# The list of pieces of a fused attention and mixer kernel, ordered anew up to the channel feed-forward

## The chip, the cores and the metric

One core of one Trainium2 chip runs the whole computation as one launch. The metric is device time in microseconds (us) of that core. The kernel before takes 791.38 us, the median of three runs (790.44, 791.38 and 794.9). The engines are TensorE (PE in the rows; PEld is its loading of weights), VectorE (DVE), ScalarE (ACT), GpSimd (POOL) and SyncE (SP). Each takes its instructions in the order in which they were issued to it. SP issues every load and store here.

## What is computed

Attention over 4 batches of 8 heads (576 tokens, 64 dimensions) in two versions, added: a local one, in which a token sees the tokens nearer than 4, and one on means of 4 neighbouring tokens, repeated back to full length. Then a gated feed-forward over 512 channels (mixer 1), a rank-32 mixing of tokens with U and V, and a channel feed-forward with 2048 hidden channels. The weights of mixer 1 and the later ones arrive in double precision.

```python
out_d = sm_attn(q_d, k_d, v_d)                      # q_d, k_d, v_d: means of 4 tokens
mask = np.abs(pos[:, None] - pos[None, :]) < factor # factor = 4
attn = softmax(np.where(mask, scale * q @ k.T, -1e9))
x = np.repeat(out_d, factor, axis=2) + attn @ v     # then heads side by side: 512 channels
h = np.maximum(x @ w_in, 0.0)                       # mixer 1, d_ff = 1024
gate = 1.0 / (1.0 + np.exp(-conv3(h)))              # 3 taps along tokens, per channel
x = h * gate @ w_out
u = x + (x.T @ U @ V).T                             # tokens mixed, rank 32
out = u + np.maximum(u @ w_ch1, 0.0) @ w_ch2        # 4 * 512 hidden channels
```

## The kernel before

The 32 heads run as 16 pairs. For a pair p, q and k are loaded (L295), transposed on TensorE against a unit matrix (L355), copied out and summed over 4 tokens (L376, L386, L407, L417). Scores S come from L441 (mask) and L447, those of the means Sd from L470; their maxima from VectorE (L454, L480), exponentials from ScalarE (L461, L489), scaling of the softmax from GpSimd or VectorE (L504). P is transposed again (L516, L520), copied out (L529, L533), and multiplied with values: L551 takes vw, the values in windows, loaded by six transfers (L305 to L307) into a buffer that there is only once; L562 takes vd, sums of vr (loaded at L316, added on GpSimd at L427). VectorE adds both into x (L583).

Mixer 1 takes x in 6 blocks of 384 tokens and 8 groups of hidden channels: 48 products "1.n" (L793, twelve matmuls each, since every operand is split in a high and a low part), a relu on ScalarE (L804), the convolution (L823 on ScalarE, L829 on VectorE), tanh (L833), the gate (L838, split at L843 and L846), and the products back "2.n" (L855). Sums are evicted at L864. Then the token mix with U and V (L889 to L910), whose inputs are split at L871 and L875, and the channel feed-forward (L962 and L981, which fill the second half of the time).

A weight block is 512 KB of doubles. It is loaded (L323 or L325 for mixer 1), decoded in four steps (ScalarE L213, VectorE L215, L217, L220), and split (high part ScalarE L225, low part GpSimd or VectorE L229). U and V are loaded and decoded the same way through one spare buffer (L741 to L777): the second half of V (L768) can only be loaded when GpSimd has read the first (L777).

What sets the order is one string of 2570 words, CFG["SEQ"], from L22 on. The loop at L1024 to L1026 reads it word by word, and each word issues one piece on all the engines that it uses: "alq.9" loads q of pair 9, "alk" its k, "alw" vw, "alv" vr, "aqT" transposes, "aS" the scores, "wl.2" loads weight block 2, "wd.2" its next decode step, "wh.2" its high part, "wo.2" its low part on GpSimd and "wO.2" the same on VectorE, "1.0" the next three matmuls of product 1.0, "r1.0" its relu, "uv" the next step of U and V, "mi" and "mo" the token mix, "3.n", "4.n" the channel feed-forward. Engines wait for each other through semaphores that the framework sets; no scheduler moves anything. A word further ahead is thus an instruction further ahead in the queue of each engine that it uses.

Of the kernel before, what the change touches and what calls it, by code (L numbers as in the profile page):

```python
# [21 lines left out]
    SEQ="wl.2 wd.2 lc C wd.2 wd.2 wl.0 wd.2 wd.0 wh.2 alk.0 wd.0 wd.0 wd.0 wh.0 alq.0 aqT.0 wo.0 alv.0 avd.0 "  # L22
# [143 lines left out]
def mixer_kernel(ctx, tc, q, k, v, w_in, conv_w, w_out, mU, mV, w_ch1, w_ch2, out, stop=9, dbg=None, early_end=False):  # L166
# [856 lines left out]
    for name, (_, fn) in OPS.items():  # L1023
        ACTS["a" + name] = fn  # L1024
    for word in CFG["SEQ"].split():
        name, *at = word.split(".")  # L1026
# [30 lines left out]
```

## Time and profile before

| what | before |
|---|---|
| device time, median of 3 runs | 791.38 us |
| profiled execution, device time | 791.73 us |
| its span in the trace | 789.5 us |
| TensorE busy | 749.0 us, 95% |
| VectorE busy | 423.5 us, 54% |
| ScalarE busy | 343.7 us, 44% |
| GpSimd busy | 168.3 us, 21% |

The span runs from the first to the last recorded instruction. Busy time is summed over an engine's instructions. In the page's 40 slices of the span the figures are busy tenths, from left to right, about 19.7 us each; the row PEclk is the granted clock of TensorE in tenths of full speed:

```profile
PE   3767999999999999999999999999999999999998
DVE  6798896977887889899866511121221212112112
ACT  4777877857767666676444211111111110111110
POOL 3456546325323314112413100000000000000000
PEclk9578999999999999999999999999999999999999
```

The first four slices are attention without a product of mixer 1. From the fifth on attention and mixer 1 run together, from 271.3 us (the first L889) with the token mix, whose last L889 starts at 380.4 us; the rest is the channel feed-forward.

### The profile page before, as it was taken

The numbers are of one execution on the slowest core, as the hardware profiler recorded it, in microseconds if no ns is written. First come the engines' busy times: TensorE is split into PE (matmuls) and PEld (weight loads), VectorE is DVE, ScalarE is ACT, GpSimd is POOL, SyncE is SP. The second block draws the span as 40 slices with busy tenths as digits, with TensorE's granted clock in tenths as the row PEclk, the third lists the DMA queues.
The fourth block names the chain that finished last, engine by engine and source line by source line (L and its number), as shares of the span: only waits on it lengthen the run. The fifth ranks groups of instructions, "written<-read, shape, count | busy, mean of one in ns | idle before, by whom it ended". The sixth has DMA issues, their size and how long they took to land.

```text
span 789.5 us, 13123 instructions
## 1 busy us (share of the span) xinstructions
PE 749.0 (95%) x5061; PEld 665.2 (84%) x5061; DVE 423.5 (54%) x830; ACT 343.7 (44%) x1029; POOL 168.3 (21%) x237
## 2 busy tenths in 40 slices
PE   3767999999999999999999999999999999999998
PEld 3556888879888898987898988999899899999997
DVE  6798896977887889899866511121221212112112
ACT  4777877857767666676444211111111110111110
POOL 3456546325323314112413100000000000000000
PEclk9578999999999999999999999999999999999999
DMA  9967644253241302121234100010010001001001
GB/s 208 218 169 176 143 104 106 48 119 75 66 108 52 97 28 80 54 81 32 70 113 160 67 2 0 1 41 1 0 41 1 1 1 40 1 1 41 1 0 41
DMA packets 85458, 51.04 MB, mean 65 GB/s; under 512 B 62716, under 2 KB 79892, under 8 KB 85396
## 3 DMA queue, kind: packets, MB, share of 16 engines
q1 hardware_dynamic: 85396, 50.21, 24.5%
q8 instruction: 40, 0.66, 0.3%
q14 instruction: 22, 0.18, 0.1%
HBM read 45.47 MB, written 4.72 MB: 64 GB/s over the span
## 4 chain that ended last, share of the span: by engine, by line
PE 84%; DVE 8%; ACT 3%; DMA 2%; SPq 1%; issue 1%; POOL 1%; DVEq 0%; POOLq 0%; ACTq 0%
PE acc L981 25%; PE gb L962 13%; PE g L962 13%; PE acc L855 11%; PE g L793 9%; PE O L551 3%; PE gb L793 2%; PE tr L355 2%; PE Sd L470 1%; DVE hc L829 1%; PE O L562 1%; PE T L516 1%; PE h L889 1%; PE ut L948 1%; DMA qr<-in_q_dram 1%
## 5 line engine op out<-in xcount | busy, mean ns | idle before, releaser
L981 PE MATMUL acc<-w,a 128*128 128x512 f32 x864 | 216.0, 393 | 0.1
L981 PEld LDWEIGHTS acc<-w,a 128*128 128x128 f32 x864 | 160.7, 188 | 29.2 <-DVE a L971 0.6
L855 PE MATMUL acc<-w,ghl 128*128 128x512 f32 x432 | 112.8, 399 | 0.1
L962 PE MATMUL gb<-uT,w 128*128 128x384 f32 x576 | 111.4, 339 | 0.0
L962 PE MATMUL g<-uT,w 128*128 128x384 f32 x576 | 111.4, 339 | 0.0
L962 PEld LDWEIGHTS gb<-uT,w 128*128 128x128 f32 x576 | 101.7, 188 | 3.8 <-DVE a L971 0.2
L962 PEld LDWEIGHTS g<-uT,w 128*128 128x128 f32 x576 | 101.6, 188 | 3.7 <-DVE a L971 0.2
L971 DVE SCALAR_TENSOR_TENSOR a<-gb,a 128x384 fp32r<-128x384 f32 x48 | 26.7, 557 | 129.4 <-ACT a L970 129.3
L855 PEld LDWEIGHTS acc<-w,ghl 128*128 128x128 f32 x432 | 80.1, 190 | 17.1 <-DVE ghl L846 1.4
L793 PE MATMUL g<-xhl,w 128*128 128x386 f32 (+1 forms) x456 | 92.9, 346 | 0.2 <-ACT hc L804 0.2
L971 DVE SCALAR_TENSOR_TENSOR a<-g,a 128x384 fp32r<-128x384 f32 x48 | 26.7, 556 | 123.0 <-ACT a L970 123.0
L793 PEld LDWEIGHTS g<-xhl,w 128*128 128x128 f32 x456 | 80.5, 191 | 2.9 <-issue 0.7
L970 ACT ACTIVATE a<-g 128x384 fp32r<-128x384 f32 x48 | 23.5, 491 | 134.0 <-PE g L962 130.1
L970 ACT ACTIVATE a<-gb 128x384 fp32r<-128x384 f32 x48 | 23.5, 490 | 132.4 <-PE gb L962 123.7
L829 DVE SCALAR_TENSOR_TENSOR hc<-hc,cw 128x384 f32<-128x384 f32 x96 | 64.4, 672 | 13.2 <-ACT hc L823 11.1
L461 ACT ACTIVATE P<-S,nm 122x64 f32<-122x64 f32 x160 | 47.8, 319 | 5.4 <-DVE nm L454 5.1
L846 POOL TENSOR_TENSOR ghl<-hc,ghl 128x384 fp32r<-128x384 f32 x22 | 25.1, 1142 | 78.2 <-ACT ghl L843 62.4
L833 ACT ACTIVATE hc<-hc 128x384 f32<-128x384 f32 x48 | 25.2, 527 | 24.3 <-DVE hc L829 24.1
L843 ACT ACTIVATE ghl<-hc 128x384 fp32r<-128x384 f32 x48 | 25.1, 527 | 22.8 <-DVE hc L838 16.2
L551 PEld LDWEIGHTS O<-PT,vw 64*64 64x64 f32 x640 | 23.5, 149 | 12.4 <-DVE xd L572 2.7
L461 ACT ACTIVATION_READ_ACCUMULATOR P<-S,nm 122x1 f32 x160 | 33.9, 212 | 0.0
L551 PE MATMUL O<-PT,vw 64*64 64x58 f32 x640 | 27.1, 237 | 7.0 <-DVE xd L572 2.4
(129 smaller groups left out, 1008.2 us busy)
## 6 DMA issues: line engine op xcount, KB each, us to landing
wraw<-in_moe_w_ch_dram SPq DMA_DIRECT2D x29, 512.0 KB
kr<-in_k_dram SPq DMA_DIRECT2D x32, 144.0 KB
qr<-in_q_dram SPq DMA_DIRECT2D x32, 144.0 KB
vr<-in_v_dram SPq DMA_DIRECT2D x32, 144.0 KB
out_dram<-u SPq DMA_DIRECT2D x17, 256.0 KB
w1t<-in_moe_w_in_dram SPq DMA_DIRECT2D x8, 512.0 KB
w1t<-in_moe_w_out_dram SPq DMA_DIRECT2D x8, 512.0 KB
vw<-in_v_dram SPq DMA_DIRECT2D x32, 128.0 KB
```

What stands on the lines that cost most here:

```text
L461: nc.scalar.activation(out=e["P"][:, i, h], in_=e["S", h][:122, i], func=AF.Exp, bias=e["nm"][:, h, i:i + 1], accum_out=e["sm"][:, i, h:h ...
L551: nc.tensor.matmul(O[rows, c:c + QB], e["vw"][rows, 2 * i + a], PT[rows, i, 64 * a:64 * a + QB], start=True, stop=True)
L793: nc.tensor.matmul(p[:, :wd], w[:, a, cc], xhl[g, cc][:, b, :wd], start=k == 0, stop=k == 3 * NCC - 1)
L829: nc.vector.scalar_tensor_tensor(out=o, in0=inner(g, hts[n], k), scalar=cw[:, k * NF + f:k * NF + f + 1], in1=o, op0=ALU.mult, op1=ALU.add)
L833: nc.scalar.activation(out=cts[n], in_=cts[n], func=AF.Tanh)
L843: nc.scalar.activation(out=t[:, 0], in_=cts[n], func=AF.Copy)
L846: eng.tensor_tensor(ghl[n][:, 1], cts.pop(n), ghl[n][:, 0].bitcast(F32), op=ALU.subtract)
L855: nc.tensor.matmul(acc[g][c], t[:, a, c * P:(c + 1) * P], w[:, b], start=f == 0 and i == 0, stop=f == NF - 1 and i == 2)
L962: nc.tensor.matmul(p[:, :TB], w[:, a, cc], uT[g, cc][:, b, :TB], start=k == 0, stop=k == 3 * NCC - 1)
L970: nc.scalar.activation(out=t[:, 0], in_=p[:, :TB], func=AF.Relu)
L971: nc.vector.scalar_tensor_tensor(out=t[:, 1], in0=p[:, :TB], scalar=0.0, in1=t[:, 0].bitcast(F32), op0=ALU.max, op1=ALU.subtract)
L981: nc.tensor.matmul(acc2[g][c], t[:, a, c * P:(c + 1) * P], w[:, b], start=f == 0 and i == 0, stop=f == NF2 - 1 and i == 2)
```

## The change

Only the string differs. It holds the same 2570 words' worth of pieces, and from word 1959 on it is the same word by word; the first 1958 stand in a new order. In some places a piece that can go to one of two engines is given to the other: GpSimd is issued 228 instructions instead of 239, VectorE 842 instead of 831, ScalarE 821 as before. By line: low parts of weights (L229) on VectorE 26 instead of 21, low parts of the gate (L846) 29 instead of 26, low parts of the token mix's inputs (L875) 12 instead of 10. Buffers, the matmuls and their number are the same. The first line of the string, and the lines with the load of pair 9's vw ("alw.9"):

```diff
-    SEQ="wl.2 wd.2 lc C wd.2 wd.2 wl.0 wd.2 wd.0 wh.2 alk.0 wd.0 wd.0 wd.0 wh.0 alq.0 aqT.0 wo.0 alv.0 avd.0 "
+    SEQ="wl.0 wd.0 wd.0 lc C alq.0 aqT.0 wd.0 wd.0 alk.0 wh.0 aqc.0 wl.2 akT.0 akv.0 aqs.0 wl.1 aks.0 wd.2 wd.2 "
...
-        "aE0.11 avd.10 aE1.11 anv.10 akc.12 c1.12 th.12 2.10 2.10 2.9 2.10 andv.11 alk.14 gh.11 gL.11 alw.9 "
+        "aEd.11 2.6 alw.9 uv 1.10 1.10 1.10 1.10 akv.12 2.7 2.7 2.7 gh.8 gl.8 r1.10 aT1.9 axdv.8 axa.8 ax.8 avd.9 "
```

In the three places below a row is a line of the program, what it issues, and the tiles (out<-in). Numbers behind a tile's name tell its copies apart.

SP's queue from its first transfer on, before and then now. w1t is a weight block of mixer 1, craw the weights of the convolution, qr and kr are q and k of a pair, vr the values for the means:

```order
L325 DMA w1t_144<-in_moe_w_in_dram 128x4x256
L688 DMA craw_139<-in_moe_conv_w_dram 24x256
L325 DMA w1t_157<-in_moe_w_in_dram 128x4x256
L295 DMA kr_163<-in_k_dram 96x6x64 x2
L295 DMA qr_171<-in_q_dram 96x6x64 x2
L316 DMA vr_182<-in_v_dram 72x2x256 x2
L323 DMA w1t_190<-in_moe_w_out_dram 128x1024
L295 DMA qr_249<-in_q_dram 96x6x64 x2
L295 DMA kr_265<-in_k_dram 96x6x64 x2
```
```order
L325 DMA w1t_144<-in_moe_w_in_dram 128x4x256
L688 DMA craw_139<-in_moe_conv_w_dram 24x256
L295 DMA qr_156<-in_q_dram 96x6x64 x2
L295 DMA kr_168<-in_k_dram 96x6x64 x2
L325 DMA w1t_174<-in_moe_w_in_dram 128x4x256
L323 DMA w1t_188<-in_moe_w_out_dram 128x1024
L316 DMA vr_201<-in_v_dram 72x2x256 x2
L295 DMA kr_209<-in_k_dram 96x6x64 x2
L295 DMA qr_212<-in_q_dram 96x6x64 x2
```

The first q and k moved ahead of the second weight block, and q ahead of k.

VectorE's queue in the same part of the program, from the eviction of the convolution's weights (cw) on. L215, L217 and L220 are the decode of a weight block; kT, qs and ks are the first pair's k and the sums over 4 tokens:

```order
L695 COPY cw_141<-cps_152 128x24
L215 TENSOR_SCALAR w1t_144<-w1t_144 128x512
L217 SCALAR_TENSOR_TENSOR w1t_144<-w1t_144 128x512
L220 SCALAR_TENSOR_TENSOR w1t_144<-w1t_144 128x512
L215 TENSOR_SCALAR w1t_157<-w1t_157 128x512
L217 SCALAR_TENSOR_TENSOR w1t_157<-w1t_157 128x512
L220 SCALAR_TENSOR_TENSOR w1t_157<-w1t_157 128x512
L407 COPY kT0_128<-tr_192 128x576
L386 TENSOR_REDUCE qs_228<-tr_174 128x144
L417 TENSOR_REDUCE ks_232<-tr_192 128x144
```
```order
L695 COPY cw_141<-cps_153 128x24
L217 SCALAR_TENSOR_TENSOR w1t_144<-w1t_144 128x512
L220 SCALAR_TENSOR_TENSOR w1t_144<-w1t_144 128x512
L407 COPY kT0_128<-tr_176 128x576
L386 TENSOR_REDUCE qs_184<-tr_159 128x144
L417 TENSOR_REDUCE ks_190<-tr_176 128x144
L215 TENSOR_SCALAR w1t_174<-w1t_174 128x512
L217 SCALAR_TENSOR_TENSOR w1t_174<-w1t_174 128x512
L229 TENSOR_TENSOR w_0_171<-w1t_144,w_0_171 128x512
L220 SCALAR_TENSOR_TENSOR w1t_174<-w1t_174 128x512
```

The decode of the second block moved behind the first pair's k and sums.

SP's queue around the two halves of V (L768, four transfers each). vw_2164 is pair 8's vw in the first fence, and vw_2524 pair 9's; in the second fence vw_2276 is pair 9's:

```order
L307 DMA vw_2164<-in_v_dram 64x8x64
L768 DMA w2t_2201<-in_moe2_V_dram 32x576 x4
L295 DMA kr_2269<-in_k_dram 96x6x64 x2
L316 DMA vr_2346<-in_v_dram 72x2x256 x2
L768 DMA w2t_2375<-in_moe2_V_dram 32x576 x4
L295 DMA kr_2518<-in_k_dram 96x6x64 x2
L305 DMA vw_2524<-in_v_dram 64x64
L306 DMA vw_2524<-in_v_dram 64x64
L307 DMA vw_2524<-in_v_dram 64x8x64
```
```order
L316 DMA vr_2237<-in_v_dram 72x2x256 x2
L295 DMA qr_2250<-in_q_dram 96x6x64 x2
L305 DMA vw_2276<-in_v_dram 64x64
L306 DMA vw_2276<-in_v_dram 64x64
L307 DMA vw_2276<-in_v_dram 64x8x64
...
L768 DMA w2t_2287<-in_moe2_V_dram 32x576 x4
L295 DMA qr_2337<-in_q_dram 96x6x64 x2
```

Pair 9's vw moved ahead of both halves of V.

## Rows read from the trace of the kernel before

**Rows 1.** The page, busy time, share of the span and instructions of each engine.

```profile
PE 749.0 (95%) x5061; PEld 665.2 (84%) x5061; DVE 423.5 (54%) x830; ACT 343.7 (44%) x1029; POOL 168.3 (21%) x237
```

**Rows 2.** Windows: us, each engine's busy time (instructions), granted clock, DMA share, GB/s.

```profile
core 0: us, PE busy (x) PEld busy (x) DVE busy (x) ACT busy (x) POOL busy (x), PEclk, DMA share, GB/s
0.00:20.00 20.00, 7.45 (x76) 6.52 (x77) 13.09 (x27) 9.54 (x25) 7.96 (x29) 1.00 1.06 208
20.00:40.00 20.00, 14.54 (x170) 12.00 (x170) 15.19 (x33) 15.04 (x68) 9.36 (x10) 0.59 0.98 213
40.00:60.00 20.00, 12.33 (x143) 10.49 (x142) 17.96 (x32) 14.22 (x55) 10.96 (x14) 0.76 0.67 169
60.00:80.00 20.00, 15.21 (x231) 12.59 (x230) 16.93 (x39) 15.87 (x67) 13.13 (x18) 0.84 0.73 172
...
225.00:370.00 145.00, 141.74 (x905) 124.09 (x905) 123.50 (x233) 100.20 (x255) 34.71 (x49) 1.00 0.21 63
...
340.00:360.00 20.00, 20.00 (x102) 17.88 (x101) 19.35 (x34) 14.76 (x29) 2.55 (x2) 1.00 0.17 53
```

**Rows 3.** TensorE's waits: line, releaser: us in total, times, longest.

```profile
PE tr L355 <- DMA qr<-in_q_dram: 4.4, 1, 4.4
...
PE h L889 <- DVE Ht L896: 3.1, 2, 1.7
PE T L516 <- DVE P L504: 3.0, 1, 3.0
...
PE O L551 <- DMA vw<-in_v_dram: 2.0, 2, 1.7
```

**Rows 4.** The chain that ended last, 0 to 90 us: start, us, what.

```profile
4.28 6.37 DMA qr<-in_q_dram
10.79 2.17 PE tr L355 x12
...
79.90 2.87 PE g L793 x12
```

**Rows 5.** The page, DMA issues: count and KB of each.

```profile
kr<-in_k_dram SPq DMA_DIRECT2D x32, 144.0 KB
...
w1t<-in_moe_w_in_dram SPq DMA_DIRECT2D x8, 512.0 KB
```

**Rows 6.** Timeline 160 to 176 us: start, us, engine, instruction, [idle before, releaser].

```profile
161.07 0.80 POOL L777 TENSOR_TENSOR Vs<-w2t,Vs 32x288 fp32r<-32x288 f32 x1 [3.32 <-ACT Vs L775]
...
161.90 2.24 SPq L768 DMA_DIRECT2D w2t<-in_moe_V_dram  x4
...
165.58 0.47 SPq L305 DMA_DIRECT2D vw<-in_v_dram  x1
...
168.72 0.62 SPq L307 DMA_DIRECT2D vw<-in_v_dram  x1
...
171.81 1.25 PE L551 MATMUL O<-PT,vw 64*64 64x58 f32 x34 [1.65 <-DMA vw<-in_v_dram]
```

**Rows 7.** Windows, the 6 us behind that wait; columns as in rows 2.

```profile
172.00:178.00 6.00, 6.00 (x63) 5.05 (x61) 3.18 (x11) 1.05 (x3) 1.26 (x1) 0.72 0.75 143
```

**Rows 8.** Groups by line and form: busy us, mean ns, idle before, releaser.

```profile
L875 POOL TENSOR_TENSOR x<-u,x 128x512 fp32r<-128x512 f32 x8 | 12.5, 1570 | 16.7 <-ACT x L871 15.8 <-PE gb L962 0.9
...
L229 POOL TENSOR_TENSOR w<-wst,w 128x512 fp32r<-128x512 f32 x6 | 8.0, 1367 | 3.0 <-ACT w L225 3.0
...
L229 DVE TENSOR_TENSOR w<-wst,w 128x512 fp32r<-128x512 f32 x10 | 6.9, 710 | 0.0
L875 DVE TENSOR_TENSOR x<-u,x 128x512 fp32r<-128x512 f32 x10 | 6.7, 682 | 0.0
```

**Rows 9.** Timeline, VectorE's decode step L217 alone, and beside GpSimd's L427.

```profile
6.98 0.69 DVE L217 SCALAR_TENSOR_TENSOR w1t<-w1t 128x512 uint32<-128x512 uint32 x1
...
29.11 2.03 POOL L427 TENSOR_TENSOR vr<-vr 72x256 f32<-72x256 f32 x2
...
29.45 1.10 DVE L217 SCALAR_TENSOR_TENSOR w1t<-w1t 128x512 uint32<-128x512 uint32 x1
```

216 rows, old and new, of the table SEQ are left out of this document.

## The prediction, made before the changed kernel was run

> **What bounds the kernel now.** I read the busy shares first: TensorE works for 749.0 of the 789.5 us of the span [rows 1]. So 40.5 us without a matmul are all that an order can remove, beside matmuls that run at a low clock. Then the windows [rows 2], for where these are. In the first 80 us TensorE is busy for 7.45 + 14.54 + 12.33 + 15.21 = 49.5 us: 30.5 of the 40.5 us lie there, in attention before the first product of mixer 1. The granted clock is 0.59, 0.76 and 0.84 in the last three of these stretches, a mix of the levels 1.2 and 2.4 GHz. VectorE is the fullest engine there (15.2, 18.0 and 16.9 of each 20 us). From 225 to 370 us TensorE is busy for 141.7 of 145 us, but VectorE is too, for 123.5; in 340:360 it has 19.35 of 20 us, and TensorE still all 20. Third, what ended TensorE's waits [rows 3]: 4.4 us for the first q, 3.1 us for Ht (one matmul waits for the eviction of the sum just before it, inside one piece, which no order of pieces changes), and 2.0 us for vw, of which 1.65 in one place. Last the chain of what ended last [rows 4]: it goes through q's transfer (6.37 us from 4.28), the transposes at 10.79, and reaches the first product at 79.90.
>
> So there are two stretches where order can pay: the 80 us until the first product, and the stall for vw at 171.8 us. The same buffers, pieces and matmuls stand on both sides, so a third term can only be new waits.
>
> **The change part by part: the start.** Before, SP issues the first W1 block, the small conv weights, a second W1 block, k and q; after, q and k come ahead of the second block. A W1 block is 512 KB, q or k twice 144 KB [rows 5]. So q's last byte stands behind 512 + 24 + 512 + 288 + 288 = 1624 KB before, behind 512 + 24 + 288 = 824 KB after. At 208 GB/s, the rate of this stretch [rows 2], these are 8.0 and 4.1 us; the transposes began at 10.79 [rows 4], 2.8 us more than 8.0, so they should begin near 6.9 now: 3.9 us earlier. How much of it arrives at 79.9 is the question, since VectorE's queue has to go through its pieces anyway. I went down the list in both orders and gave each instruction the mean of its group: ahead of the last part of the first product stand VectorE 63.6, ScalarE 66.5, GpSimd 34.9 and TensorE 39.2 us before; 63.3, 65.0, 31.1 and 38.8 after. On VectorE and ScalarE that is the same work within 1.5 us. Its order has changed too: VectorE now evicts the first k ahead of the second block's decode, three instructions. Two ends: 3.9 us if the head start is held to the end, nothing if VectorE's queue is as late as before; below nothing, GpSimd now scales pair 0's P, for which TensorE already waited 3.0 us [rows 3] while VectorE did it. If GpSimd is as much slower there as in the subtraction of [rows 8], 1.57 against 0.68, and one more piece follows it onto the path, up to 2 us are lost. VectorE idles for 6.9 of the first 20 us and for 9.9 of the following 60 [rows 2], so about half of its late work hangs on something other than its own queue: I take **−2.0 us**, range −3.9 to +2.
>
> **The vw stall.** Pair 9's vw is six transfers of SP, and they are issued from 165.58 to 168.72 us, since the four loads of V's second half stand ahead of them [rows 6]. These waited until GpSimd had read the first half (Vs at 161.07 for 0.80), then took 2.24 us to issue; SP's queue is in order, so k and vw stood behind. TensorE meets the gap at 171.81 and waits 1.65 us, 6.2 us after the first of the six issues. After it the clock falls: 0.72 granted on average from 172 to 178 us [rows 7], where TensorE is busy all 6 us; (1 − 0.72) × 6 = 1.7 us. In the new order pair 9's vw stands ahead of both halves of V. It then waits only for its own buffer (the product of pair 8 with it). By the same list of means, 10.6 us of matmuls lie between that issue and pair 9's product, against 6.2 needed: the wait goes with 4 us to spare. What is queued behind it now is V, which only the token mix uses, from word 1223 of the list; this vw is word 664. Gain 1.65 + 1.7 = **−3.4 us**; end 0, if another wait stands at once behind it.
>
> **New waits.** Elsewhere the order loses some slack. Pair 15's vw is issued 5.9 us of matmuls ahead of its use, against 6.2 needed: 0.3. The low part of the last token-mix input is made by GpSimd right ahead of the matmul that takes it: 1.57 against 0.68 us on VectorE [rows 8], 0.9 more. A channel weight's low part does the same at 1.37 against 0.71 [rows 8], 0.7 more. Sum **+1.9 us**; lower end 0 (each can be hidden by matmuls that are queued between), upper end +6, worked out under the second rival. In all GpSimd gets 11 instructions fewer and VectorE 11 more; by the means of their groups that is 12.7 us off GpSimd and 7 us onto VectorE. I price it at nothing beyond the above because TensorE ran through 340:360 with VectorE at 97%.
>
> Two rows touch a rule. VectorE's decode step took 1.10 us where a GpSimd addition ran beside it for 2.03 us, and 0.69 us with none beside it [rows 9]. The Trainium skill, "SBUF — State Buffer", section "SBUF: two separate sides", says that VectorE and GpSimd share a port pair as an exclusive lock, so that when a VectorE operation with two inputs in SBUF meets a GpSimd one that reads SBUF, whichever starts second is blocked for the whole instruction. By that rule the 12.7 us taken off GpSimd could give VectorE more back than the 7 us that it gets, and the new order would be lighter on VectorE. The rows show a stretch of 0.4 us for VectorE rather than a block of 2 us, so the sum doesn't use it.
>
> **Sum.** −2.0 − 3.4 + 1.9 = −3.5 us on a span of 789.5 us: 786.0. The profiled execution took 791.73 us, 2.2 us more than its span, and 0.35 over the median of 791.38; so 788.2 us, and 788 beside the median. A measurement of this kernel tells about 0.5% from no change, that is 787.4 and 795.3.
>
> **Rivals.** *More is won.* The head start is held (−3.9), vw gives 3.4, no new wait shows: −7.3, so 784.4; and with fewer meetings of GpSimd and VectorE in the first 80 us, 11 × 0.4 = 4.4 us more at most, 780. For it: 30 us of TensorE's idle time lies there, and some of it is waits for pieces of VectorE, like the 3.0 us for P [rows 3]. Against: the work ahead of the first product is nearly the same. The rule of the skill named above is on its side.
>
> *VectorE becomes the bound in the second half of mixer 1: slower.* By the same sums, the pieces up to the relu of product 1.40 (331.9 us in the trace) came to 293.3 us of TensorE and 274.7 of VectorE; now to 293.6 and 284.6. So 9.9 us more of VectorE's work stands ahead of the same products. From 225 to 370 us it idles for 145 − 123.5 = 21.5 us; if 9.9 of these can be filled, nothing is lost, and that is the point from which it decides. If none can (they are waits in chains between ScalarE and VectorE), TensorE waits all 9.9 and then runs a while at the lower clock, another 1.7: −2.0 − 3.4 + 11.6 = +6.2, so 797.9. Half of the 11.6 is the +6 above. For it: VectorE stood at 97% in 340:360. Against: there TensorE didn't wait [rows 2].
>
> *The time stays.* The start gives nothing since VectorE's queue sets the first product, and vw's 3.4 us are eaten by three or four new waits of about 1 us, like those priced above: about 791.
>
> **How the numbers follow.** The forecast (786 to 790.5, 788 the middle) gets 0.37, more won 0.27, the time stays 0.16, VectorE the bound 0.20. Faster by over 0.5%: all of "more" and a third of the forecast, 0.27 + 0.13 = 0.40. Slower by over 0.5%: most of VectorE's case, 0.17. The rest, 0.43, is within. The range reaches from 781, with most of "more" in it, to 797, which takes in the larger part of VectorE's case; not quite 0.2 is left out. The forecast's own range is 786 to 790.5.
>
> **What would show it.** Right: the first transposes near 7 us; the first product between 76 and 80; no wait for vw near 170 us, and the clock at 1.00 there; waits of TensorE after 84 us of 6 to 8 us in all, 3.1 of them for Ht. More won: the first product before 76. VectorE the bound: waits of TensorE for ghl or for pieces of VectorE between 280 and 370 us, and a clock under 1.00 in these windows. The time stays: the first product at 79 to 80, and new waits of about 1 us each from 84 us on. What would make all of it wrong is a wait that the list of means can't see, above all a buffer held longer in the new order that stalls SP's queue for several transfers at once.

## The result, and the profile after

The changed kernel takes 783.21 us, the median of four runs (781.88 to 787.33); the kernel before takes 793.03 in the same comparison. The ratio is 0.9876, with a 95% interval from 0.9849 to 0.9903: 9.8 us faster, 7.7 to 12.0. The profiled execution took 782.97 us, with a span of 781.2 us, 8.3 less than before.

The page, the busy line that answers [rows 1]:

```profile
PE 745.9 (95%) x5061; PEld 665.1 (85%) x5061; DVE 433.6 (56%) x841; ACT 341.1 (44%) x1029; POOL 160.4 (21%) x226
```

TensorE is without a matmul for 781.2 − 745.9 = 35.3 us instead of 40.5, and its matmuls themselves take 3.1 us less, at a mean clock that is a little higher (0.98 against 0.975). VectorE works 10.1 us more and GpSimd 7.9 less.

The windows that answer [rows 2]; the columns are the same:

```profile
0.00:20.00 20.00, 8.76 (x103) 7.70 (x107) 14.57 (x28) 8.96 (x24) 9.66 (x29) 1.00 0.96 209
20.00:40.00 20.00, 16.11 (x166) 12.99 (x157) 14.26 (x33) 15.47 (x71) 9.49 (x12) 0.51 0.83 183
40.00:60.00 20.00, 14.30 (x185) 12.29 (x183) 17.77 (x37) 14.76 (x56) 7.37 (x9) 0.72 0.62 159
60.00:80.00 20.00, 17.05 (x252) 14.32 (x251) 19.29 (x47) 17.25 (x77) 13.52 (x21) 1.00 0.96 206
...
225.00:370.00 145.00, 141.58 (x879) 125.35 (x875) 125.47 (x235) 96.25 (x232) 36.38 (x52) 1.00 0.22 66
```

TensorE works 56.2 of the first 80 us instead of 49.5. From 60 to 80 us its clock is at 1.00 where it was 0.84, with VectorE at 19.29 of 20 us. From 225 to 370 us TensorE is as full as before, 141.58 against 141.74 us, and waits only for Ht (3.2 us) and once for vw (0.2).

The first 100 us in two stretches, first before, then after:

```profile
0.00:37.00 37.00, 18.99 (x210) 15.63 (x212) 25.72 (x53) 21.77 (x75) 15.93 (x37) 0.81 1.03 212
37.00:100.00 63.00, 50.11 (x602) 43.58 (x599) 53.83 (x115) 51.02 (x205) 34.69 (x44) 0.84 0.70 165
```
```profile
0.00:37.00 37.00, 21.88 (x218) 18.12 (x220) 28.04 (x58) 22.80 (x89) 18.09 (x38) 0.78 0.96 210
37.00:100.00 63.00, 53.52 (x702) 46.05 (x701) 54.80 (x125) 51.39 (x213) 31.93 (x43) 0.89 0.74 167
```

Up to 37 us TensorE is idle for 2.9 us less than before, at a slightly lower clock. From 37 to 100 us it is idle for 9.5 us instead of 12.9, at a mean clock of 0.89 instead of 0.84: 702 matmuls (of several sizes) instead of 602 in the same 63 us. Four places on the way in the kernel after: the first transposes, the first P of pair 0, the product of pair 1 with its values, the last nine matmuls of product 1.0.

```profile
6.97 1.22 PE L355 MATMUL tr<-ident,qr 96*128 96x96 f32 x6
...
26.70 0.88 PE L516 MATMUL T<-ident,P 122*128 122x122 f32 x3 [1.65 <-POOL P L504]
...
51.98 2.39 PE L551 MATMUL O<-PT,vw 64*64 64x58 f32 x40 [2.42 <-ACT xd L572]
...
73.97 2.11 PE L793 MATMUL g<-xhl,w 128*128 128x386 f32 x9
```

Before, the transposes began at 10.79 [rows 4], and the next two places were

```profile
27.05 0.85 PE L516 MATMUL T<-ident,P 122*128 122x122 f32 x3 [3.04 <-DVE P L504]
...
54.88 2.39 PE L551 MATMUL O<-PT,vw 64*64 64x58 f32 x40 [1.26 <-ACT xd L572]
```

Product 1.0 ended at 79.90 + 2.87 = 82.8 [rows 4]; now its first three matmuls start at 69.7, and it ends at 76.1. So the transposes are 3.8 us ahead, pair 0's P only 0.35, pair 1's product 2.9, product 1.0 is 6.7. A single place does not tell the whole lead, since the pieces around it differ: when pair 0's last product with its values starts (36.6 us before, 36.75 now), TensorE now has pair 3's transposes behind it, some 2 us of work that stood after that product before.

The second place, pair 9's vw, which answers [rows 6]:

```profile
144.14 0.47 SPq L305 DMA_DIRECT2D vw<-in_v_dram  x1
...
148.11 2.07 SPq L768 DMA_DIRECT2D w2t<-in_moe_V_dram  x4
```
```profile
153.72 0.41 PE L551 MATMUL O<-PT,vw 64*64 64x58 f32 x8
154.88 0.72 PE L562 MATMUL O<-PTd,vd 72*64 72x144 f32 x8 [0.75 <-ACT PTd L533]
```

vw is issued 9.6 us ahead of its use instead of 6.2, ahead of both halves of V, and no wait for it stands there. What stands there is a wait of 0.75 us for a copy by ScalarE. Past 100 us, TensorE's waits in the kernel after (line, releaser: us in total, times, longest):

```profile
PE h L889 <- DVE Ht L896: 3.2, 2, 1.8
PE O L551 <- ACT Pd L489: 0.8, 1, 0.8
PE O L562 <- ACT PTd L533: 0.8, 1, 0.8
PE acc L855 <- POOL ghl L846: 0.7, 1, 0.7
PE g L793 <- ACT hc L804: 0.6, 2, 0.3
```

With three more of 0.3, 0.3 and 0.2 us, all but Ht's come to 3.7 us. Before, there were 2.5 us beside Ht's, 2.0 of them for vw. From 84 us on, where the prediction counted, the waits come to 7.7 us with Ht's.

### The profile page after: what moved, and what is told of

Its sections match the earlier page's. It is cut to its first block, busy times and chain, and to the rows that moved or that the text cites. A ratio compares the mean times of both kernels' runs of the same rounds, so it can differ in the third digit from the quotient of the medians.

```text
span 781.2 us, 13125 instructions
## 1 busy us (share of the span) xinstructions
PE 745.9 (95%) x5061; PEld 665.1 (85%) x5061; DVE 433.6 (56%) x841; ACT 341.1 (44%) x1029; POOL 160.4 (21%) x226
## 4 chain that ended last, share of the span: by engine, by line
PE 79%; DVE 9%; ACT 5%; issue 2%; POOL 2%; DMA 2%; SPq 1%; DVEq 0%; ACTq 0%; POOLq 0%
PE acc L981 25%; PE gb L962 13%; PE g L962 13%; PE acc L855 9%; PE g L793 6%; PE O L551 3%; PE gb L793 2%; PE tr L355 1%; DVE hc L829 1%; PE h L889 1%; ACT Pd L489 1%; PE O L562 1%; PE Sd L470 1%; DVE hc L838 1%; PE ut L948 1%
## 5 line engine op out<-in xcount | busy, mean ns | idle before, releaser
L829 DVE SCALAR_TENSOR_TENSOR hc<-hc,cw 128x384 f32<-128x384 f32 x96 | 60.8, 638 | 6.0 <-ACT hc L823 4.2
L846 POOL TENSOR_TENSOR ghl<-hc,ghl 128x384 fp32r<-128x384 f32 x19 | 21.1, 1113 | 90.0 <-ACT ghl L843 75.9
L838 DVE SCALAR_TENSOR_TENSOR hc<-hc 128x384 f32<-128x384 f32 x48 | 29.3, 614 | 7.7 <-ACT hc L833 7.5
```

The source lines that it names most:

```text
L829: nc.vector.scalar_tensor_tensor(out=o, in0=inner(g, hts[n], k), scalar=cw[:, k * NF + f:k * NF + f + 1], in1=o, op0=ALU.mult, op1=ALU.add)
L838: nc.vector.scalar_tensor_tensor(out=o, in0=o, scalar=1.0, in1=inner(g, hts.pop(n), 1), op0=ALU.add, op1=ALU.mult)
```

## Experiments

I set out with three theories on the 9.8 us: O, that the start's gain comes from the order of the pieces between about 37 and 80 us; H, that it is the head start of q and k; C, that it is the choice of engines. L (the distance between a load and its decode) and S (how long the new order has to go on) came with the first results.

All runs compute everything; a time is set against runs of the kernel before in the same comparison (medians 792.8 to 793.3). Differences in us are those of the ratio; the difference of the two medians lies up to 1.2 us beside it. In the kernels of the experiments the string takes more lines, so that a line of the program has a number 27 higher. Most of them are made of a stretch of one order and the rest in the other. Five words of one piece stand for what the lists of before and after write as one (aE00.5 to aE04.5 for aE0.5). The pieces of the first stretch are left out of the second list, and engines are chosen as in the list that a piece comes from.

**The head start alone.**

```diff
-wl.2 wd.2 lc C wd.2 wd.2 wl.0 wd.2 wd.0 wh.2 alk.0 wd.0 wd.0 wd.0 wh.0 alq.0 aqT.0
+wl.2 wd.2 lc C alq.0 alk.0 wd.2 wd.2 wl.0 wd.2 wd.0 wh.2 wd.0 wd.0 wd.0 wh.0 aqT.0
```

> The kernel before with one move: the first q and k are loaded ahead of the second weight block, as in the changed kernel; everything else stands as before. Theory O (the gain of the start comes from the order of pieces between about 37 and 80 us, and the head start is used up by then): transposes near 7 us, first scaled P at 26.5 to 27, no change of the time, 0 +- 1.5 us against before. Theory H (the head start is what is held): faster by 3.9 to 6 us. Theory C (the choice of engines, fewer meetings of GpSimd and VectorE): 0.

Measured: 792.39 us, ratio 0.998 (0.996 to 1.000), so 1.6 us faster, 0 to 3.2. TensorE's timeline:

```profile
6.64 1.22 PE L382 MATMUL tr<-ident,qr 96*128 96x96 f32 x6
...
28.18 0.84 PE L543 MATMUL T<-ident,P 122*128 122x122 f32 x3 [3.28 <-DVE P L531]
```

The transposes are 4.1 us ahead of the kernel before, and pair 0's P is 1.1 us behind it. What the transposes gain is waited for again at P. ScalarE's first step on the second block now starts at 10.11 us instead of 7.70, and the decode of that block still stands ahead of the first pair's k and sums, where the changed kernel has moved it behind them. So theory H falls for the early loads alone; early loads with the decode moved behind were not run by themselves.

**The new order until the first product, and its mirror.**

```diff
 and.4 aEd.5 alk.7 1.0 1.0 1.0
-r1.0 an.4 c0.0 akT0.7 aks.7 akc.7 akT1.7 aks.7 aqT0.7 aqsa.7 aqc.7 wl.12 wd.12
+wl.12 wd.12 wd.12 wd.12 wd.12 wh.12 an.4 akT0.7 aks.7 akv.7 wl.13 wd.13 wd.13
```

> The new order up to the last part of product 1.0 (321 of 2670 pieces), then the remaining pieces in the order and with the engines of before. Theories O and H: first product done near 76 us, as in the changed kernel, the wait for vw near 170 us still there: faster than before by 6 to 7 us. Theory C: only the choices of the first 80 us count, so faster by 2 to 3.

Measured: 792.25 us, ratio 0.9989 (0.9975 to 1.0002). None of the 6 us came. Yet the lead was there: product 1.0 ended at 73.83 + 2.11 = 75.9 us, as early as in the changed kernel. Then TensorE waited:

```profile
73.83 2.11 PE L820 MATMUL g<-xhl,w 128*128 128x386 f32 x9
...
81.64 0.67 PE L543 MATMUL T<-ident,P 122*128 122x122 f32 x2 [5.21 <-POOL P L531]
```

The chain of what ended last shows why (start, us, what):

```profile
71.71 5.56 DMA w1t<-in_moe_w_in_dram
...
77.35 0.67 ACT w1t L240
...
79.23 0.69 DVE w1t L247
...
80.33 1.27 POOL P L531
```

At the seam, weight block 12 is loaded and decoded in one breath. Its transfer takes 5.56 us, ScalarE's and VectorE's queues stand at the decode, and the softmax of pair 4 stands behind that. A lead of 6 us was given back in one wait.

The mirror:

```diff
 1.0 wd.13 wd.13 1.0 1.0 1.0
-wO.12 aE10.5 aE11.5 aE12.5 aE13.5 aE14.5 alq.7 wl.14 r1.0 and.5
+aE10.5 aE11.5 aE12.5 aE13.5 aE14.5 alq.7 r1.0 c0.0 akT1.7 aks.7 aqT0.7 aqsa.7
```

> The mirror: the order of before up to the last part of product 1.0, then the remaining pieces in the new order. Theories O and H: first product near 82.5 us as before, no wait for vw beyond 1 us near 170 us, clock 1.00 there, so faster than before by 1.5 to 3.5 us. Theory C, since nearly all choices lie behind the first product: faster by 5 or more.

Measured: 790.19 us, ratio 0.9957 (0.9937 to 0.9978), 3.4 us faster, 1.7 to 5.0, as expected of the vw term by theories O and H, and less than theory C asked (the interval just reaches its 5).

**The new order with the old engines.** Two of the 163 words, in the changed kernel and then in this run:

```diff
-wl.1 aks.0 wd.2 wd.2 wd.2 wO.0 wd.1 wd.2 wh.2 wo.2 alv.0
+wl.1 aks.0 wd.2 wd.2 wd.2 wo.0 wd.1 wd.2 wh.2 wO.2 alv.0
```

> The new order, but each piece that can go to one of two engines goes to the one it had before (163 words differ). Theories O and H: within 2 us of the changed kernel, so faster than before by 8 to 11. Theory C: the gain is gone, within 2 us of before, and VectorE's decode steps are stretched beside GpSimd as before.

Measured: 840.8 us, ratio 1.0602 (1.0579 to 1.0625): 48 us slower than before, which no theory had. TensorE's longest sums of waits past 80 us:

```profile
PE acc L882 <- DVE ghl L873: 7.3, 3, 4.2
PE O L589 <- POOL vd L455: 6.1, 4, 2.8
PE O L578 <- DMA vw<-in_v_dram: 6.0, 2, 4.3
```

The order goes with the engines chosen for its pieces; with 163 of them on the other one, new waits stand in many places. This tells that order and engines go together, and nothing on whether GpSimd and VectorE hinder each other.

**The seam mended.** In the run that lost its lead at the seam, the decode of block 12 and the first steps of block 13 moved back:

```diff
-wl.12 wd.12 wd.12 wd.12 wd.12 wh.12 an.4 akT0.7 aks.7 akv.7 wl.13 wd.13 wd.13 wO.12 wl.14 r1.0 and.5
+wl.12 an.4 akT0.7 aks.7 akv.7 wl.13 wl.14 r1.0 and.5 aqT0.7 aT1.4 aT0.4 aT2.4 wd.12 wd.12 wd.12 wd.12
```

> The new order up to the last part of product 1.0 and the old one behind it, as in the run before with that name, but the decode of weight block 12 no longer stands right behind its load: its pieces and the first two of block 13 are moved some 20 words back. Theory L (the lead at the first product is real, and was given back because a decode stood in the queues while its load was under way, with the softmax of pair 4 behind it): the 5.2 us wait of TensorE for P near 80 us is gone or under 1.5 us, and the kernel is faster than before by 4.5 to 6.5 us. Rival (the old order behind the first product can't use a lead, since VectorE and ScalarE set the pace there until 100 us): the lead melts in several small waits between 76 and 110 us, faster than before by 0 to 2 us.

Measured: 793.73 us, ratio 1.0001 (0.9975 to 1.0026). The wait for P fell to 0.9 us, but two others stood in its place:

```profile
79.54 2.72 PE L820 MATMUL g<-xhl,w 128*128 128x386 f32 x9
...
87.79 0.47 PE L382 MATMUL tr<-ident,kr 96*128 96x96 f32 x3 [2.35 <-ACT PT L556]
...
90.66 0.74 PE L382 MATMUL tr<-ident,qr 96*128 96x96 f32 x3 [2.41 <-DVE qs L413]
```

The time is the rival's. The trace can't show why: it is of the slowest of the twelve executions (798.85 us), and in it product 1.0 ended at 79.54 + 2.72 = 82.3 us, so there was hardly a lead to lose (the last section shows where it went).

**Loads further ahead in the old order, and late in the new one.** Blocks 6 to 13, of which this is one:

```diff
-aE01.3 aE02.3 aE03.3 aE04.3 aM1.3
...
-aks.4 wl.10 wd.10 aPVb.1
+aE01.3 aE02.3 aE03.3 wl.10 aE04.3 aM1.3
...
+aks.4 wd.10 aPVb.1
```

> The order of before with one kind of move: the loads of weight blocks 6 to 13, of which seven stand one or two pieces ahead of their first decode step, stand 20 pieces further ahead. Theory L: ScalarE's waits for weight blocks after 40 us go, the first product is done 4 to 6 us earlier, and the kernel is faster by 3 to 6 us. Rival O (it is the order of the attention pieces on VectorE, ScalarE and GpSimd that makes the lead, not the loads): first product earlier by 0 to 2 us, kernel within 2 us of before; it may lose by q and k that now stand behind the blocks.

Measured: 796.72 us, ratio 1.0037 (1.0017 to 1.0056): 2.9 us slower. ScalarE's waits for weight blocks past 30 us are gone (2.5 us before), and TensorE's for q come to 6.6 us in two places instead of 4.4 in one. That is neither theory's number; theory L as the sole cause falls.

In the new order, blocks 3 to 11 put back beside their decode:

```diff
-ac2.1 wl.6 wl.7 aks.3 ab1.1 aqT.4 alw.1 wd.6 aqc.4
+ac2.1 aks.3 ab1.1 aqT.4 alw.1 wl.6 wd.6 aqc.4
```

> The new order with the loads of weight blocks 3 to 11 put back right ahead of their first decode step, as they stood before (6 to 29 pieces later than in the new order). Theory L: the first product is done 4 us or more later, and the kernel loses 4 to 8 of its 9.8 us. Rival O: it loses 0 to 2 us.

Measured: 797.93 us, ratio 1.0052 (1.0024 to 1.0080), 4.1 us slower than before and some 14 behind the changed kernel. ScalarE and TensorE:

```profile
47.44 0.66 ACT L240 ACTIVATE w1t<-w1t 128x512 f32<-128x512 f32 x1 [5.22 <-DMA w1t<-in_moe_w_in_dram]
```
```profile
51.02 1.75 PE L497 MATMUL Sd<-ks,qdbd 128*96 128x144 f32 x6 [5.46 <-ACT P L488]
```

The same picture as at the seam: 5.2 us of ScalarE's queue for a block, then 5.5 us of TensorE. The block's load was issued only at 43.64 us, behind the six transfers of a vw, and took 3.72 us. So the loads' place is needed for the new order, though it doesn't help the old one.

**vw alone, in the old order.**

```diff
-aT2.9 gL.9 uv uv 1.11 akc.12
...
-andv.11 alk.14 gh.11 gL.11 alw.9 aPVa.9
+aT2.9 gL.9 uv alw.9 uv 1.11 akc.12
...
+andv.11 alk.14 gh.11 gL.11 aPVa.9
```

> The order of before with pair 9's vw moved ahead of the second half of V, and nothing else. Prediction's term: the wait for vw near 171 us goes, the clock stays at 1.00 from 172 to 178 us, faster than before by 3.4 us (2 to 4). Rival (the wait is moved: V or k behind it come late): under 1 us.

Measured: 792.05 us, ratio 0.997 (0.995 to 0.999): 2.4 us faster, 0.8 to 4.0 (the two medians are 1.2 us apart). The wait is gone, and the clock is at 1.00 behind its place; columns as in rows 2:

```profile
172.00:178.00 6.00, 5.52 (x71) 4.14 (x70) 5.35 (x15) 3.89 (x22) 0.41 (x1) 1.00 0.63 125
```

**How far the new order has to go.** To about 100 us, 480 pieces:

```diff
 akT0.9 alv.7 2.1 1.4 avd.7 aqc.9
-gl.2 c1.3 th.3 anv.7 wd.13 wd.13 1.4 akc.9 1.4 1.4
+wd.13 wd.13 wO.12 wd.13 alq.10 wd.13 wl.15 wd.15 alv.6 avd.6
```

> The new order for 480 of the 2670 pieces (to about 100 us, behind product 1.3), the old one behind it. Theory S (the lead at the first product holds only if the order of the next 30 us is the new one too, which decodes weight blocks 12 to 15 later; then it holds): faster than before by 5 to 7 us, the wait for vw near 165 us still there. Rival (the lead needs the new order all the way to the token mix): faster by 0 to 2 us.

Measured: 799.79 us, ratio 1.0084 (1.0056 to 1.0111), 6.7 us slower than before. TensorE and ScalarE:

```profile
116.28 0.85 PE L547 MATMUL T<-ident,Pd 96*72 96x96 f32 x4 [6.98 <-DVE ks L444]
```
```profile
113.29 0.66 ACT L240 ACTIVATE w1t<-w1t 128x512 f32<-128x512 f32 x1 [4.98 <-DMA w1t<-in_moe_w_out_dram]
```

Again the seam: wl.15 loads a weight block, wd.15 decodes it right behind. ScalarE's queue stands for 4.98 us, VectorE's decode steps follow, and behind them ks, for which TensorE waits. The next two words, alv.6 and avd.6, do the same to GpSimd: it waits 8.5 us for vr, and TensorE 3.4 us more. This run says nothing on theory S but where its seam lies. In its trace product 1.0 ended only at 81.4 us, too.

To the piece ahead of vw, 723 pieces:

```diff
 alq.12 aPVa.8 aEd.11 2.6
-alw.9 uv 1.10 1.10 1.10 1.10 akv.12 2.7 2.7 2.7
+aqT0.12 aqv.12 aqs.12 alq.14 2.7 uv uv px.2.0
```

> The new order for 723 pieces, up to the piece ahead of the load of pair 9's vw, the old one behind it, in which that load stands behind the second half of V. Theory S: faster than before by 5 to 7 us; the wait for vw near 165 us is there. Rival: the lead is lost at the seam, 0 to 2 us.

Measured: 786.75 us, ratio 0.9915 (0.9893 to 0.9938): 6.7 us faster, 4.9 to 8.5, with a wait for vw of 1.6 us left. This is the start's term, with a seam that costs little, and theory S as expected; between 84 us and vw the kernel before had only 1.2 us of waits and a clock of 1.00, so nearly all of it must come from the first 84 us.

Past vw's use, 800 pieces:

```diff
 2.8 2.8 2.9 c1.11 th.11 c1.10
-1.12 2.9 2.9 alk.13 1.12 1.12 1.12 th.10 gt.10 gh.10
+alv.10 th.10 gt.10 gh.10 gL.10 1.12 1.12 1.12 1.12 gt.11
```

> The new order for 800 pieces, past the product of pair 9 with its vw, the old one behind it. Theory S: the start's 5 to 7 us and 2 to 3 us for vw, together 8 to 10 faster than before, as the changed kernel or better by up to 2 us, since the new order's small waits between 180 and 300 us stay out. Rival: slower than the changed kernel by 2 us or more.

Measured: 788.25 us, ratio 0.9939 (0.9918 to 0.9959), 4.8 us faster, 5 behind the changed kernel: the rival's side. Two seam waits stand in the trace, 1.48 us ending at 172.54 and 2.71 us ending at 178.88 (for ScalarE, ahead of the next transposes), behind a chain through a transfer and V's decode.

One piece more than 723, the load of vw:

```diff
 alq.12 aPVa.8 aEd.11 2.6 alw.9
-uv 1.10 1.10 1.10 1.10 akv.12 2.7 2.7 2.7 gh.8
+aqT0.12 aqv.12 aqs.12 alq.14 2.7 uv uv px.2.0
```

> One piece more of the new order than in the run that ended ahead of the load of pair 9's vw: 724 pieces, so that this load stands ahead of both halves of V, and the old order behind it. Theory S (start and vw add up, the rest of the new order gives nothing): 6.7 us for the start and 2.4 for vw, 9.1 us faster than before, within 1.5 us of the changed kernel, and no wait for vw over 1 us near 165 us. Rival 1 (the new order's later part costs some 2 us in small waits): 2 us faster than the changed kernel. Rival 2 (the vw term needs the rest of the new order too): no gain over the 6.7 us.

Measured: 787.77 us, ratio 0.9927 (0.9898 to 0.9955), 5.8 us faster, 3.6 to 8.1, on the side of rival 2; theory S's 9.1 is outside. The wait for vw is gone. In the trace, which is of the slowest of the six executions (790.97 us), a wait of 2.24 us ends at 84.56, where the order is still the new one, and another stands a few us ahead of vw's place:

```profile
159.08 3.80 PE L820 MATMUL g<-xhl,w 128*128 128x388 f32 x12 [1.88 <-ACT hc L831]
```

## Why the prediction was right, and where it was not

The direction and the range held: 783.2 us lies in 781 to 797, though under the forecast's own 786 to 790.5. The forecast of 788 saw 3.5 us of a gain of 9.8. By its steps:

**What bounds the kernel** was read rightly. Both gains lie in the two stretches that the windows and waits named, the first 80 us and vw.

**The start** is the term that was mis-sized: −2.0, range −3.9 to +2, and 6.7 us measured (4.9 to 8.5 in the run that has the new order up to vw). Its first half was exact: transposes at 6.97 us, forecast 6.9. The step that failed is the next one, that the head start is the most the start can give, and that equal work ahead of the first product speaks for little more. At pair 0's P 0.35 us of the head start were left, and the early loads alone gave 1.6 us (0 to 3.2). The price feared there didn't come: with GpSimd scaling P, TensorE's wait for it fell from 3.04 to 1.65 us. What the start gave is idle time taken from the whole of the first 100 us, 2.9 us up to 37 us and 3.4 behind, and a higher clock from 60 us on, with the same work in another order. The sum of work in a queue is only a floor: from 37 to 100 us before, VectorE was idle for 63 − 53.83 = 9.2 us, ScalarE for 12.0 and TensorE for 12.9. I had read such idle time, but used it only to halve the head start. The bound to take was TensorE's idle time of the first 100 us. How much of the 6.7 us the clock gave, and whether it rose because the waits were gone, is not shown.

**vw**: the mechanism was right. The load stands ahead of V, the wait and the low clock are gone. The size was 3.4, and 2.4 (0.8 to 4.0) alone in the old order; in the run with 724 pieces it gave nothing on top of the start. The part that looks too large is the clock: in the run with only the head start, the same wait is there and the clock stays at 1.00 behind it. Timeline and window of that run, and the 6 us behind the same wait (1.53 us) in the run with the seam mended:

```profile
171.42 1.25 PE L578 MATMUL O<-PT,vw 64*64 64x58 f32 x34 [1.53 <-DMA vw<-in_v_dram]
```
```profile
172.00:178.00 6.00, 6.00 (x62) 5.38 (x59) 3.90 (x14) 1.87 (x6) 1.26 (x1) 1.00 0.71 146
```
```profile
179.30:185.30 6.00, 6.00 (x63) 5.02 (x60) 3.30 (x11) 1.16 (x3) 1.26 (x1) 0.72 0.78 147
```

Seven traces have this wait, of 1.1 to 1.65 us. Behind it the clock was 0.72 in two of them (the kernel before and the seam mended) and 1.00 in five. So the 1.7 us of [rows 7] come in some executions only; at two in seven they are worth 0.5 us, an estimate, and 1.65 + 0.5 is near the 2.4 measured.

**New waits**: forecast 1.9 us at three places. Of the three only pair 15's vw shows a wait in the trace, 0.19 us at 253.45 where 0.3 were priced. 3.5 us stand elsewhere, against 0.5 before beside vw's. The sign of 6 to 8 us past 84 us came (7.7), but from other places. What they cost is open: if start and vw add up, 6.7 + 2.4 = 9.1 leave 0.7 of the 9.8 us, less than the intervals; in the run with 724 pieces they did not add up (5.8). The mirror, with all of the new order behind the first product, gained 3.4, no less than vw's 2.4.

**The rivals.** "More is won", 784.4, came nearest, and its sign, the first product before 76, came as well (it starts at 69.7 and ends at 76.1), but not by its reasons. The early loads alone gave little. Fewer meetings of GpSimd and VectorE show nothing on the decode steps with two inputs: in the first 80 us L217 took 783 ns on average before (13 times) and 729 after (12), but L220 took 728 and 778, together 756 and 754. My reading of [rows 9] was wrong, too: the 2.03 us are two additions. Two such take 1.43 us nearly undisturbed (132.03 us in that trace), so the first, begun at 29.11, had some 0.4 us left when L217 came at 29.45, just what L217 took longer. That is no sign against a block. Three rows of the trace after, in which L229 makes the low part of a weight:

```profile
14.46 0.68 DVE L217 SCALAR_TENSOR_TENSOR w1t<-w1t 128x512 uint32<-128x512 uint32 x1
...
14.51 1.77 POOL L229 TENSOR_TENSOR w<-w1t,w 128x512 fp32r<-128x512 f32 x1 [3.02 <-ACT w L225]
...
15.18 1.66 DVE L220 SCALAR_TENSOR_TENSOR w1t<-w1t 128x512 uint32<-128x512 uint32 x1
```

L229, which takes 1.27 us with nothing of VectorE beside it (11.04 us in the trace before), starts just behind L217 and takes 0.5 us longer; L220 starts in the middle of L229 and takes 1.0 us longer than its 0.69, ending 0.56 us after L229. By the rule of the Trainium skill, "SBUF — State Buffer", section "SBUF: two separate sides", of a VectorE operation with two inputs in SBUF and a GpSimd operation that reads SBUF, the one that starts second is blocked until the other is through. These rows agree with it. What the engines' choice gave to the time is open all the same, since the run that gave the engines back broke the order. By the means 7 us were to come onto VectorE and 12.7 off GpSimd; 10.1 and 7.9 did. VectorE as the bound did not come: TensorE lost nothing from 225 to 370 us with 2 us more of VectorE's work there. "The time stays" had the start at nothing, which fits the early loads alone (0 to 3.2 us), and was wrong on the rest.

**What stays open** is which part of the order of the first 100 us makes the 6.7 us. It isn't the loads' distance alone (2.9 us slower in the old order), nor the early q and k alone, and the first 321 pieces alone gave nothing. What is shown is that the gain is there with the first 723 pieces and not with 321 or 480. Whether the new order itself is needed past 100 us, or only a seam at which no load stands beside its decode, is not shown: both shorter runs lost their time at such a seam, and the mended one had no lead in its trace.

## What to carry to other kernels

An order is worth what its worst seam leaves of it: in three of the runs a load stood right ahead of its first consumer in an in-order queue, and TensorE lost 5 to 7 us in one wait (5.2, 5.5 and 7.0). So a load belongs at least its issue-to-landing time (3.7 to 5.6 us in these three) ahead of the first instruction that wants it, on every queue that this instruction blocks. That alone is no gain: the kernel before has most of its loads beside their decode as well, and moving them ahead made it 2.9 us slower. And a gain in a stretch bounded by several engines in turn is bounded by the idle time there, not by the queue's work, which hardly changes.

## What the runs showed of the hardware that was not expected

The start of one and the same order differs between executions. ScalarE's first decode step of the second weight block, in two runs whose first 321 pieces are the same (the run to the first product, and that with the seam mended):

```profile
9.58 0.66 ACT L240 ACTIVATE w1t<-w1t 128x512 f32<-128x512 f32 x1
```
```profile
11.82 0.66 ACT L240 ACTIVATE w1t<-w1t 128x512 f32<-128x512 f32 x1 [2.16 <-DMA w1t<-in_moe_w_in_dram]
```

The block landed at least 2 us later, and pair 1's product followed at 54.27 instead of 51.83 us, product 1.0 ended at 82.3 instead of 75.9. The clock differs as well: with the same order up to 160 us, 60 to 80 us had 0.84 in the trace of before and 0.50 in that of the run with vw moved alone:

```profile
60.00:80.00 20.00, 18.92 (x195) 15.71 (x194) 16.88 (x36) 14.93 (x60) 11.89 (x16) 0.50 0.68 156
```

Over all traces with the old order up to product 1.0 (before, head start, vw alone, mirror), that product ended at 81.7 to 85.6 us, with the clock at 0.50 to 0.87 from 60 to 80 us. In the seven with the new order it ended at 75.9 to 77.3 us in five, with the clock at 0.97 to 1.00, and at 81.4 and 82.3 in two (480 pieces and the seam mended), with the clock at 0.76 and 0.78. So the lead is there in most of these traces of the new order, not in all. Why it fails in the run with 480 pieces, whose second block landed in time (decode from 9.63 us), is open.

The kernel before ran from 789.8 to 798.5 us over its runs. A difference of 2 or 3 us in the first 80 us between two traces is thus no evidence by itself; for a time, only medians with intervals are.
